# Attention, spectral mixing and two MLPs on one core: block 0's operand and the first weight half built in the query part

## The chip, the cores and the metric

One core of a Trainium2 chip runs the whole program in one launch. The metric is the device time in microseconds (us) of that core. TensorE (PE) multiplies 128x128 weights with up to 512 columns, and its weight loads (PEld) run beside the products; VectorE (DVE), ScalarE (ACT) and GpSimd (POOL) work elementwise; SyncE (SP) issues most of the DMAs.

## The reference

The inputs are q, k, v of 4 batches, 8 heads, 576 tokens and 64 features. Three parts follow one another:

```
phi(x) = exp(h - max h) / sqrt(m),  h = x omega^T - |x|^2/2
attn   = (phi(q) (phi(k)^T v)) / (phi(q) sum phi(k) + 1e-6)
x  = attn, heads joined: 4 x 576 x 512
u  = x + real(fft over tokens and features of x)
un = (u - mean u) / sqrt(var u + 1e-6)
x  = u + relu(un w1a) w2a          w1a: 512x2048, w2a: 2048x512
u  = x + (tokens mixed by U V, rank 32)
out = u + relu(u w1b) w2b
```

All inputs are float32, and the products are made from float32 values split into a high and a low part (hi, lo), three products for one: hi.hi, lo.hi, hi.lo.

## The kernel before

The tokens stand in `uT`, 128 partitions (features) by 4 feature groups by 2304 tokens. A first loop (L907) has 46 steps `n`. Steps 0 to 17 are batches 0 and 1, steps 18 to 35 batches 2 and 3; of each 18, the first nine are key tiles (`proj`, `exps`, `kvmm`) and the last nine query tiles of 128 tokens (`qtr`, `num`, `xdiv`, `xtr`). `xdiv` divides by the denominators into `x` and writes a strided copy `xr`; `xtr` transposes it into `uT` one or two steps later. `split_in(n+3)` (L239) splits the inputs of three steps ahead into `thi` and `tlo`.

The transform of a batch is written into the same steps as pieces, by the table `PLAN` (L58): F is a fold (sums and differences of pairs of `x` tiles, then four half sums, then a split into `zh` and `zl`, where the copies and subtractions wait in the list `zpend` until `zflush`), L the fold of the shared tile, S a stage of products with cosine tables whose result is split into `abh`, `abl`, D the second stage, whose results are added into `uT` by POOL (L443). A letter g or v after a fold names the engine of its sums, of its half sums and of its `zl`.

The first MLP works on five blocks of tokens (512, 384, 512, 384, 512). A block needs its mean, its centred operand `X[(0, blk)]` as a hi and a lo tile, and the factor `RST[blk]` of its variance, which multiplies only the result. For block 0 the mean and variance are made by `ln_stats` from step 23 on, the operand by `ln_apply` (L569) in step 36: for each of four feature groups a subtraction `n` (L575), a copy `xh` (ACT, L120) and a subtraction `xl` (L121), with the engines of `LNA`. The tiles lie in a pool `xpa` that opens in step 36, where the query part's pools close. The other blocks go by generators in the list `jobs`: `prep_lna` makes the mean (`s`, `pmn`), `prep_lnb` (L607) the operand, then the variance: squares summed on POOL (L626), tiny products `pvc` (L640), root, reciprocal, products `prs`, `RST`. Each `yield` ends a tick, and `tick()` advances the first generator of `jobs` by one. `l1` and `l2` call it after every feature group, that is, every three products of a unit.

A unit is one block and 128 hidden columns: `l1(i)` makes twelve products `ph`, ReLU on ACT (`hh`) and the rest on DVE (`hl`); `l2(i)` makes twelve products into `acc`. The weights come as 64-bit integers' halves, are converted (`w_conv_a`, `conv_b`) into `W[j]`, j = 2 x column group + half, and split into `wh`, `wl` by `wsplit` (L192); `w_conv_a(j)` also issues the load of half j+1 on SP.

Steps 36 to 45 still belong to the first loop. Step 36 (s = 0) opens the pools of the MLP, calls `ln_apply(0)` and splits the first halves of weights 0 and 1 on DVE; step 37 calls `l1(0)`, splits five more halves on POOL, converts halves 6 and 7 and puts `prep_lna(1)`, `prep_lnb(1)` into `jobs`; from step 38 on `step(s - 2)` runs a unit each. After the loop all jobs are drained, `prep_lnb(2)` runs until its operand stands, and units 7 to 159 follow.

In the first loop a planner orders the instructions of each engine by its own simulation, with the program's order as priority; `tc.issue_after(i)` puts the instructions made in it, on the engine of `i`, behind `i`. From unit 7 on (`manual_schedule`) each engine runs in the order of the program.

Of the kernel before, what the change touches and what calls it, by code (L numbers as in the profile page):

```python
# [47 lines left out]
LNA = 'gvvgvgvg'  # L48
# [27 lines left out]
        (13, "aF0evvv aF0ovvg"),  # L76
# [17 lines left out]
def tile_favor_fnet_moe(ctx: ExitStack, tc: tile.TileContext, qT, kT, v1, om, w1a, w2a, uu, vv, w1b, w2b, cs, cd, out):  # L94
# [24 lines left out]
    def split(dst_hi, dst_lo, src, lo_eng):  # L119
        nc.scalar.activation(dst_hi, src, AF.Copy)  # L120
        lo_eng.tensor_tensor(out=dst_lo, in0=src, in1=dst_hi.bitcast(F32), op=ALU.subtract)  # L121
# [70 lines left out]
    def wsplit(fi, k, e=nc.gpsimd):  # L192
# [3 lines left out]
        pool = wpools[0 if slot < 4 else 1]  # L196
# [9 lines left out]

    ca = ExitStack()
# [7 lines left out]
    NS = 36  # L215
    raw_, hl_, vt_, phi_, pj_, kvp_, kv_, qpT_, pn_, x_, xr_ = ({} for _ in range(11))
# [56 lines left out]
    def exps(n, g):  # L273
        if n >= NS:
            return
        pss, mx = pj_[n]
        for hh in range(4):
            h = 4 * g + hh
            nc.scalar.activation(phi_[n][:, h, :], pss[g][:, hh, :], AF.Exp, bias=mx[:, h : h + 1])  # L279
# [83 lines left out]
    def fold(src, key, eng, zeng):  # L363
        z = plf.tile([128, 4, 128], F32, tag="z", name=f"z{key}", bufs=2)
        e2 = lnt("sa", f"e2{key}")[:, 0:256]
# [26 lines left out]
    def s_stage(b, kd, kind):  # L392
# [16 lines left out]
        split(abh[:, :, c0 : c0 + w], abl[:, :, c0 : c0 + w], pv, nc.vector)  # L409
# [55 lines left out]
    def zflush(k=9):  # L465
        for _ in range(min(k, len(zpend))):
            zpend.pop(0)()
# [94 lines left out]
    def x_tiles(nm, blk):  # L562
        nb = BLKS[blk][1]
        pool = xps[0 if blk < 2 else 1]
# [4 lines left out]
    def ln_apply(blk, seng, eng):  # L569
# [3 lines left out]
        for r in range(4):  # L573
            c = lnt("ct", f"n{blk}_{r}")[:, 0:nb]
            seng[r].tensor_tensor(out=c, in0=uT[:, r, c0 : c0 + nb], in1=mean, op=ALU.subtract)  # L575
            split(hi[:, r, :], lo[:, r, :], c, eng[r])
# [8 lines left out]
    def prep_lna(blk):  # L585
# [4 lines left out]
        s2 = lnt("sb", f"s2_{blk}")[:, 0:nb]  # L590
# [4 lines left out]
        for _ in range(5 if blk > 2 else 2):  # L595
# [11 lines left out]
    def prep_lnb(blk):  # L607
# [24 lines left out]
        X[(0, blk)] = hi, lo  # L632
        yield
        for _ in range(5):
# [210 lines left out]
    jobs, wjobs = [], []  # L845
# [8 lines left out]
    def tick():  # L854
        turn[0] += 1
        advance(jobs)
        if turn[0] % 2 or len(wjobs) > 2:
            advance(wjobs)

    def step(i):  # L860
# [3 lines left out]
        if i == TAIL:  # L864
            jobs.append(lnb2)
# [41 lines left out]
    for n in range(NS + 10):  # L907
        s = n % 18
        pieces = fill.get(n, [])
        if n < NS:  # L910
# [10 lines left out]
            split_in(n + 3)  # L921
            if n == LNS:
# [35 lines left out]
        else:  # L958
            if s == 0:
# [10 lines left out]
                ln_apply(0, [eng[e] for e in LNA[0:4]], [eng[e] for e in LNA[4:8]])  # L970
                wsplit(0, 0, nc.vector)
                wsplit(1, 0, nc.vector)
            if s == 1:
                xtr(n - 2)
                l1(0)
                wsplit(0, 1)
                wsplit(1, 1)
                wsplit(2, 0)
                wsplit(2, 1)
                for j in (6, 7):  # L980
                    conv_b(*w_conv_a(j), nc.gpsimd)
# [115 lines left out]
```

## Time and profile before

| | us |
|---|---|
| median of 3 runs | 1080.05 |
| lowest, highest | 1078.63, 1084.92 |
| profiled execution, its time | 1079.91 |
| its span | 1078.1 |
| mean granted clock of PE | 0.991 |

The span goes from the first instruction to the last; the time around it is 1.8 us more. The granted clock is a share of the full 2.4 GHz; the other level is 1.2 GHz, so a stretch that shows 0.66 ran part of the time at the one and part at the other. "A <- B: 1.9, 1, 1.9" in a list of waits says that A waited for B, 1.9 us in total, once, at most 1.9 us. Spans on POOL are rough.

### The profile page before, as it was taken

How to read it: one execution, taken by the hardware profiler on the slowest of the kernel's cores; microseconds unless marked ns; L12 is line 12 of the kernel's file. 1: busy time of each engine (PE TensorE's matmuls, PEld its weight loads, DVE VectorE, ACT ScalarE, POOL GpSimd, SP SyncE). 2: the span in 40 equal slices, each digit the busy share in tenths (PEclk: the TensorE clock that was granted, in tenths of full speed). 3: DMA queues.
4: the chain of work that ended last, by engine and by line, in shares of the span. 5: the costliest groups of instructions: out<-in, count | busy, mean ns of one | idle time of the engine just before them, and what ended most of it. 6: DMA issues, size and time to landing. Idle time of an engine off the chain costs nothing.

```text
span 1078.1 us, 14786 instructions
## 1 busy us (share of the span) xinstructions
PE 1048.5 (97%) x5704; PEld 925.8 (86%) x5704; DVE 582.0 (54%) x1023; ACT 400.2 (37%) x894; POOL 414.3 (38%) x386
## 2 busy tenths in 40 slices
PE   8999998889889999999999999999999999999998
PEld 7989998679788889898889787789898989888996
DVE  6798788785488653445336656562433334332222
ACT  7877786543344231322222435331312132131110
POOL 2467755765436434634445246230410140131000
PEclk9999998989999999999999999999999999999999
DMA  7642320100012120111011101111111011100111
GB/s 241 195 143 54 105 60 1 40 1 1 1 59 84 48 87 21 40 59 49 30 40 59 40 1 40 39 40 40 40 43 56 20 46 52 59 1 1 69 40 69
DMA packets 47590, 56.87 MB, mean 53 GB/s; under 512 B 3040, under 2 KB 39264, under 8 KB 47392
## 3 DMA queue, kind: packets, MB, share of 16 engines
q1 hardware_dynamic: 47232, 53.23, 15.9%
q0 software_dynamic: 288, 2.70, 0.7%
q8 instruction: 45, 0.74, 0.3%
q14 instruction: 25, 0.20, 0.1%
HBM read 51.20 MB, written 4.72 MB: 52 GB/s over the span
## 4 chain that ended last, share of the span: by engine, by line
PE 87%; DVE 6%; POOL 4%; issue 1%; ACT 1%; DMA 0%; DVEq 0%; SPq 0%; POOLq 0%; ACTq 0%
PE ph L775 12%; PE ph L777 12%; PE ph L776 12%; PE acc L796 12%; PE acc L798 11%; PE acc L797 11%; PE kvp L290 3%; PE pn L327 2%; PE pj L263 1%; POOL uT L443 1%; PE pj L264 1%; PE pj L265 1%; PE pt L311 1%; POOL s L626 1%; PE mt L710 1%
## 5 line engine op out<-in xcount | busy, mean ns | idle before, releaser
L782 DVE SCALAR_TENSOR_TENSOR hl<-ph,hh 128x512 fp32r<-128x512 f32 (+1 forms) x160 | 101.9, 637 | 360.1 <-ACT hh L781 359.7
L781 ACT ACTIVATE hh<-ph 128x512 fp32r<-128x512 f32 (+1 forms) x160 | 88.9, 555 | 509.1 <-PE ph L777 508.7
L796 PE MATMUL acc<-hh,wh 128*128 128x512 f32 (+1 forms) x640 | 238.5, 373 | 0.0
L798 PE MATMUL acc<-hl,wh 128*128 128x512 f32 (+1 forms) x640 | 237.1, 371 | 0.5 <-DVE hl L782 0.5
L797 PE MATMUL acc<-hh,wl 128*128 128x512 f32 (+1 forms) x640 | 236.9, 370 | 0.0
L808 POOL TENSOR_TENSOR uT<-uT,t 128x512 f32<-128x512 f32 (+1 forms) x80 | 99.2, 1271 | 136.5 <-DVE t L807 136.5
L158 POOL TENSOR_TENSOR w<-mc,sc 128x512 uint32<-128x512 uint32 x48 | 62.9, 1310 | 213.6 <-DVE mc L155 206.9
L798 PEld LDWEIGHTS acc<-hl,wh 128*128 128x128 f32 x640 | 120.5, 188 | 17.5 <-DVE hl L782 1.4
L796 PEld LDWEIGHTS acc<-hh,wh 128*128 128x128 f32 x640 | 120.7, 189 | 17.1 <-issue 0.9
L797 PEld LDWEIGHTS acc<-hh,wl 128*128 128x128 f32 x640 | 120.7, 189 | 15.5
L775 PE MATMUL ph<-xh,wh 128*128 128x512 f32 (+1 forms) x320 | 122.3, 382 | 0.0
L776 PE MATMUL ph<-xl,wh 128*128 128x512 f32 (+1 forms) x320 | 119.9, 375 | 1.9 <-DVE xl L121 1.9
L777 PE MATMUL ph<-xh,wl 128*128 128x512 f32 (+1 forms) x320 | 119.7, 374 | 0.5 <-DVE wl L121 0.5
L775 PE MATMUL ph<-yh,wh 128*128 128x512 f32 (+1 forms) x320 | 118.7, 371 | 0.0
L777 PE MATMUL ph<-yh,wl 128*128 128x512 f32 (+1 forms) x320 | 118.6, 371 | 0.0
L776 PE MATMUL ph<-yl,wh 128*128 128x512 f32 (+1 forms) x320 | 118.5, 370 | 0.0
L834 POOL TENSOR_TENSOR wl<-w,wh 128x512 fp32r<-128x512 f32 x56 | 75.7, 1371 | 75.2 <-ACT wh L832 64.4
L279 ACT ACTIVATE phi<-pj,mx 128x128 f32<-128x128 f32 x288 | 82.2, 385 | 10.9 <-DVE mx L268 10.1
L776 PEld LDWEIGHTS ph<-xl,wh 128*128 128x128 f32 x320 | 60.8, 190 | 10.6 <-DVE xl L121 2.4
L775 PEld LDWEIGHTS ph<-xh,wh 128*128 128x128 f32 x320 | 60.8, 190 | 9.4 <-issue 1.4
L777 PEld LDWEIGHTS ph<-xh,wl 128*128 128x128 f32 x320 | 60.8, 190 | 9.1 <-DVE wl L121 0.8
L777 PEld LDWEIGHTS ph<-yh,wl 128*128 128x128 f32 x320 | 60.1, 188 | 8.2
(644 smaller groups left out, 1765.6 us busy)
## 6 DMA issues: line engine op xcount, KB each, us to landing
raw<-in_w1a_dram SPq DMA_DIRECT2D x16, 512.0 KB, 3.6
raw<-in_w2a_dram SPq DMA_DIRECT2D x16, 512.0 KB, 3.5
raw<-in_w1b_dram SPq DMA_DIRECT2D x16, 512.0 KB, 3.6
raw<-in_w2b_dram SPq DMA_DIRECT2D x16, 512.0 KB, 3.6
vt<-in_v_dram SPq DMA_DIRECT2D x18, 260.0 KB, 4.2
raw<-in_qT_dram SPq DMA_DIRECT2D x18, 256.0 KB, 3.2
raw<-in_kT_dram SPq DMA_DIRECT2D x17, 256.0 KB, 3.1
out_dram<-uT SPq DMA_DIRECT2D x11, 256.0 KB, 2.2
```

Source lines behind the costliest of these rows:

```text
L158: aeng.tensor_tensor(out=dst.bitcast(U32), in0=mu, in1=s, op=ALU.add)
L279: nc.scalar.activation(phi_[n][:, h, :], pss[g][:, hh, :], AF.Exp, bias=mx[:, h : h + 1])
L775: nc.tensor.matmul(ph, wh[:, c], xh[:, r, :], start=(r == 0), stop=False)
L776: nc.tensor.matmul(ph, wh[:, c], xl[:, r, :], start=False, stop=False)
L777: last[0] = nc.tensor.matmul(ph, wl[:, c], xh[:, r, :], start=False, stop=(r == 3)).ins
L781: nc.scalar.activation(hh, ph, AF.Relu)
L782: nc.vector.scalar_tensor_tensor(out=hl, in0=ph, scalar=0.0, in1=hh.bitcast(F32), op0=ALU.max, op1=ALU.subtract)
L796: nc.tensor.matmul(a[r], wh[:, c], hh, start=(q == 0), stop=False)
L797: nc.tensor.matmul(a[r], wl[:, c], hh, start=False, stop=False)
L798: last[0] = nc.tensor.matmul(a[r], wh[:, c], hl, start=False, stop=(q == GRP - 1)).ins
L808: nc.gpsimd.tensor_tensor(out=u, in0=u, in1=t, op=ALU.add)
L834: nc.gpsimd.tensor_tensor(out=lo, in0=src, in1=hi.bitcast(F32), op=ALU.subtract)
```

## The change

Block 0's operand, and the first weight half of slot 0, get a pool `xp0` of their own that is open from the start. `ln_apply` becomes a generator that does one feature group in each of steps 30 to 33, all on POOL; `wsplit(0, 0)` runs in step 34 on POOL. `l1(0)` moves from step 37 to the end of step 36, and `wsplit(1, 0)` from step 36 to 37. The conversion of halves 6 and 7 and the splits of weight 3 move to step 38, with their DVE part behind the last `abl`. One fold of batch 2 moves from step 31 on DVE to step 30 on POOL, and `zflush` issues behind the last exponential. Two scratch sums change their buffers (`sq`, two of them, in place of `sa` and `sb`, one each). For blocks 3 and 4, `prep_lna` pauses three ticks before its sums and three more after them. The variance of a block becomes a generator of its own, `prep_rs`, in a second list `jobs2`, that is advanced beside `jobs`, with 9 pauses in place of 6.

```diff
-LNA = 'gvvgvgvg'
+LNA = 'gggggggg'
...
-        (13, "aF0evvv aF0ovvg"),
+        (12, "aF0oggg"),
+        (13, "aF0evvv"),
...
     def wsplit(fi, k, e=nc.gpsimd):
...
-        pool = wpools[0 if slot < 4 else 1]
+        pool = xp0 if slot + k == 0 else wpools[0 if slot < 4 else 1]
...
+    xp0 = ctx.enter_context(tc.tile_pool(name="xp0", bufs=1))
     ca = ExitStack()
...
-        e2 = lnt("sa", f"e2{key}")[:, 0:256]
+        e2 = lnt("sq", f"e2{key}")[:, 0:256]
...
-    def zflush(k=9):
-        for _ in range(min(k, len(zpend))):
-            zpend.pop(0)()
+    def zflush():
+        with tc.issue_after(lexp[0]) if n + 1 < NS else ExitStack():
+            while zpend:
+                zpend.pop(0)()
...
     def x_tiles(nm, blk):
         nb = BLKS[blk][1]
-        pool = xps[0 if blk < 2 else 1]
+        pool = xp0 if blk == 0 else xps[0 if blk < 2 else 1]
...
     def ln_apply(blk, seng, eng):
...
         for r in range(4):
+            yield
             c = lnt("ct", f"n{blk}_{r}")[:, 0:nb]
...
     def prep_lna(blk):
...
-        s2 = lnt("sb", f"s2_{blk}")[:, 0:nb]
+        s2 = lnt("sq", f"s2_{blk}")[:, 0:nb]
+        for _ in range(3 if blk > 2 else 0):
+            yield
...
-        for _ in range(5 if blk > 2 else 2):
+        for _ in range(8 if blk > 2 else 2):
             yield
...
         X[(0, blk)] = hi, lo
-        yield
-        for _ in range(5):
+        jobs2.append(prep_rs(blk, s3))
+        yield
+
+    def prep_rs(blk, s3):
+        nb = BLKS[blk][1]
+        for _ in range(9):
             yield
...
     def tick():
         turn[0] += 1
         advance(jobs)
+        advance(jobs2)
...
         if i == TAIL:
-            jobs.append(lnb2)
+            jobs.insert(0, lnb2)
...
             split_in(n + 3)
+            if n == 29:
+                lna0 = ln_apply(0, [eng[e] for e in LNA[0:4]], [eng[e] for e in LNA[4:8]])
+                next(lna0)
+            if 29 < n < 34:
+                next(lna0, None)
+            if n == 34:
+                wsplit(0, 0)
...
-                ln_apply(0, [eng[e] for e in LNA[0:4]], [eng[e] for e in LNA[4:8]])
-                wsplit(0, 0, nc.vector)
-                wsplit(1, 0, nc.vector)
             if s == 1:
                 xtr(n - 2)
-                l1(0)
-                wsplit(0, 1)
-                wsplit(1, 1)
-                wsplit(2, 0)
-                wsplit(2, 1)
-                for j in (6, 7):
-                    conv_b(*w_conv_a(j), nc.gpsimd)
-                wsplit(3, 0)
-                wsplit(3, 1)
+                if 1:
+                    wsplit(1, 0, nc.vector)
+                    wsplit(0, 1)
+                    wsplit(1, 1)
+                    wsplit(2, 0)
+                    wsplit(2, 1)
                 jobs.extend([prep_lna(1), prep_lnb(1)])
             zflush()
             for p in pieces:
                 p()
+            if s == 0:
+                l1(0)
+            if s == 2:
+                with tc.issue_after(labl[0]):
+                    for j in (6, 7):
+                        conv_b(*w_conv_a(j), nc.gpsimd)
+                wsplit(3, 0)
+                wsplit(3, 1)
...
-    while jobs:
+    while jobs or jobs2:
         tick()
```

Here `lexp` is the last exponential made and `labl` the last `abl`.

## Rows read from the trace of the kernel before

**Rows 1.** The page's first part: busy time, share of the span and instructions of each engine.

```profile
PE 1048.5 (97%) x5704; PEld 925.8 (86%) x5704; DVE 582.0 (54%) x1023; ACT 400.2 (37%) x894; POOL 414.3 (38%) x386
```

**Rows 2.** Busy time by stretch: stretch, length, engines (count), PE's granted clock, DMA, GB/s.

```profile
155.00:190.00 35.00, 31.98 (x257) 30.35 (x255) 28.92 (x73) 24.05 (x66) 16.44 (x20) 0.90 0.01 2
...
150.00:190.00 40.00, 36.98 (x297) 34.94 (x296) 33.22 (x87) 29.01 (x78) 16.98 (x21) 0.91 0.01 2
190.00:215.00 25.00, 19.96 (x108) 16.60 (x106) 17.92 (x32) 12.88 (x26) 20.57 (x21) 0.93 0.13 42
...
226.00:236.00 10.00, 7.26 (x23) 5.82 (x22) 8.53 (x18) 3.60 (x6) 6.48 (x8) 0.66 0.00 0
...
270.00:281.00 11.00, 7.97 (x36) 6.31 (x35) 3.53 (x6) 0.86 (x2) 7.01 (x7) 0.84 0.00 0
...
300.00:340.00 40.00, 36.77 (x187) 31.88 (x187) 38.23 (x55) 19.28 (x35) 21.51 (x15) 1.00 0.29 85
```

**Rows 3.** What PE's products waited for, whole span: total us, times, longest us.

```profile
PE pvc L640 <- POOL s L626: 7.1, 3, 3.0
...
PE pt L311 <- ACT phi L279: 3.6, 3, 1.6
PE ph L776 <- DVE xl L121: 1.9, 1, 1.9
PE ps_3o L402 <- DVE abl L121: 1.8, 1, 1.8
...
PE pmn L598 <- DVE s L594: 1.4, 1, 1.4
...
PE pdq2r L425 <- DVE den L336: 0.7, 1, 0.7
```

**Rows 4.** A wait of ACT in 190 to 215 us.

```profile
ACT xh L120 <- PE pn L327: 1.4, 1, 1.4
```

**Rows 5.** POOL's groups by shape in 190 to 236: busy us, mean ns, idle before.

```profile
L121 POOL TENSOR_TENSOR wl<-w,wh 128x512 fp32r<-128x512 f32 x6 | 9.0, 1514 | 0.0
...
L121 POOL TENSOR_TENSOR xl<-n,xh 128x512 fp32r<-128x512 f32 x2 | 2.6, 1282 | 1.9 <-ACT xh L120 1.9
L575 POOL TENSOR_TENSOR n<-uT,mean 128x512 f32<-128x512 f32 x1 | 1.7, 1732 | 0.0
```

**Rows 6.** POOL's groups by shape in 155 to 190.

```profile
L386 POOL TENSOR_TENSOR eo_1e<-x,x 128x512 f32<-128x512 f32 x1 | 1.3, 1271 | 0.4 <-DVE z2o L367 0.4
L575 POOL TENSOR_TENSOR n<-uT,mean 128x512 f32<-128x512 f32 x1 | 1.3, 1262 | 0.0
L367 POOL TENSOR_TENSOR z2l<-x 128x256 f32<-128x256 f32 x1 | 0.8, 789 | 0.1
...
L366 POOL TENSOR_TENSOR e22o<-eo_1o 128x256 f32<-128x256 f32 x1 | 0.7, 723 | 0.3 <-DVE z2o L369 0.3
...
L369 POOL TENSOR_TENSOR z2o<-e22o 128x128 f32<-128x128 f32 x1 | 0.4, 445 | 0.0
```

**Rows 7.** DVE in order of time: start us, duration us, line, instruction.

```profile
161.50 0.39 DVE L367 TENSOR_TENSOR z2e<-eo_0e 128x256 f32<-128x256 f32 x1
...
166.40 1.51 DVE L367 TENSOR_TENSOR z2o<-eo_0o 128x256 f32<-128x256 f32 x1
...
169.32 0.68 DVE L268 TENSOR_REDUCE mx<-pj 128x4 f32<-128x512 f32 x1
```

**Rows 8.** POOL in order of time, beside the DVE rows above.

```profile
166.15 1.47 POOL L246 TENSOR_TENSOR tlo<-raw,thi 128x512 fp32r<-128x512 f32 x1
```

**Rows 9.** POOL in order of time, first and last ahead of `pvc` of block 1.

```profile
218.34 1.45 POOL L626 TENSOR_TENSOR s<-s,q 128x384 f32<-128x384 f32 x1 [2.66 <-ACT q L624]
...
226.22 2.70 POOL L626 TENSOR_TENSOR s<-s,q 128x384 f32<-128x384 f32 x2
```

**Rows 10.** The chain that ended last, 180 to 345: start us, us, what.

```profile
264.23 4.77 POOL uT L443 x7
...
285.04 0.23 PE ph L776
```

More of the change, by code (lines that the diff above doesn't have):

```diff
@@ L119, in split @@
     def split(dst_hi, dst_lo, src, lo_eng):
-        nc.scalar.activation(dst_hi, src, AF.Copy)
-        lo_eng.tensor_tensor(out=dst_lo, in0=src, in1=dst_hi.bitcast(F32), op=ALU.subtract)
+        hi = nc.scalar.activation(dst_hi, src, AF.Copy).ins
+        return hi, lo_eng.tensor_tensor(out=dst_lo, in0=src, in1=dst_hi.bitcast(F32), op=ALU.subtract).ins
     def conv_a(dst, raw, c0, n, p, nm):
@@ L215, in tile_favor_fnet_moe @@
     NS = 36
+    lexp, lxh, labl = [None], [None], [None]
     raw_, hl_, vt_, phi_, pj_, kvp_, kv_, qpT_, pn_, x_, xr_ = ({} for _ in range(11))
@@ L278, in exps @@
             h = 4 * g + hh
-            nc.scalar.activation(phi_[n][:, h, :], pss[g][:, hh, :], AF.Exp, bias=mx[:, h : h + 1])
+            lexp[0] = nc.scalar.activation(phi_[n][:, h, :], pss[g][:, hh, :], AF.Exp, bias=mx[:, h : h + 1]).ins
     def kvmm(n):
@@ L408, in s_stage @@
         pv = ps[:, 0 : 2 * w].rearrange("p (a s) -> p a s", a=2)
-        split(abh[:, :, c0 : c0 + w], abl[:, :, c0 : c0 + w], pv, nc.vector)
+        labl[0] = split(abh[:, :, c0 : c0 + w], abl[:, :, c0 : c0 + w], pv, nc.vector)[1]
     DST = {
@@ L573, in ln_apply @@
         for r in range(4):
+            yield
             c = lnt("ct", f"n{blk}_{r}")[:, 0:nb]
             seng[r].tensor_tensor(out=c, in0=uT[:, r, c0 : c0 + nb], in1=mean, op=ALU.subtract)
-            split(hi[:, r, :], lo[:, r, :], c, eng[r])
+            lxh[0] = split(hi[:, r, :], lo[:, r, :], c, eng[r])[0]
         X[(0, blk)] = hi, lo
@@ L827, in sjob @@
         slot = fi % RING
-        pool = wpools[0 if slot < 4 else 1]
+        pool = xp0 if slot + k == 0 else wpools[0 if slot < 4 else 1]
         hi = pool.tile([128, 512], F32R, tag=f"wh{slot}_{k}", name=f"wh{fi}_{k}")
@@ L844, in tile_favor_fnet_moe @@
                 wq_at.setdefault(PER * g + 15 + q, []).append(lambda fi=GRP * (g + 1) + q, k=k: sjob(fi, k))
-    jobs, wjobs = [], []
+    jobs, jobs2, wjobs = [], [], []
     turn = [0]
```

## The prediction

> **What bounds the kernel now.** I read the page's first part, then busy time by stretches, then what TensorE (PE) waits for, then the stretches around those waits. PE is busy 97% of the span [rows 1], so the program is worth what PE loses by standing still or by running at half clock. A stretch loses its length minus its busy time, plus its length times (1 minus the granted clock). By the table of stretches [rows 2] that is, in us: A, 150 to 190, the end of the query part: 3.0 idle + 0.09 x 40 = 3.6 of clock = 6.6. B, 190 to 215, the first weight units: 5.0 + 0.07 x 25 = 1.8, 6.8. C, 226 to 236: 2.7 + 0.34 x 10 = 3.4, 6.1. D, 270 to 281: 3.0 + 0.16 x 11 = 1.8, 4.8. E, 300 to 340: 3.2, no clock. Together 27.5; what is lost elsewhere the edits don't touch. The clock of a whole stretch is a mix of 1.2 and 2.4 GHz; in A, C and D the low level stands right behind a gap of PE, so I count it with the gap.
>
> The reader should next see who ends these gaps. `pvc` (L640) waits 7.1 us in three places for the squares' sum `s` on POOL (L626): the longest, 3.0, is D's whole idle time, C's is 2.7, which leaves 1.4 for E. The transposes `pt` wait 3.6 for the exponentials, the longest, 1.6, in A; in B it is `ph` for `xl` (1.9), `ps_3o` for `abl` (1.8), `pdq2r` (0.7); in E also `pmn` for the sum `s` (1.4) [rows 3]. PE takes its instructions in order, so each of these held everything behind it.
>
> **The change, part by part.** The profiled execution took 1079.9 us around a span of 1078.1; the runs' median is 1080.05, 0.1 above. The sum is made against 1079.9.
>
> *B: the operand and first weight half built early, +4.0.* Before, `xh`/`xl` of block 0 live where the query part's tiles lay: the first ACT copy waits 1.4 us for the last `pn` product [rows 4], and four subtractions, four copies, four `xl` and the first `wl` crowd behind it. The new home is free all along, so the chain runs in steps 30 to 33 and 34, and l1(0), now one step earlier, finds its operands. From this stretch POOL loses two `xl` of 1.3 and one `n` of 1.7 [rows 5], DVE one `n`, two `xl` and one `wl`. The sums of block 1 and folds get their own `sq` buffers in place of `sa`/`sb`, which can only remove waits. The conversion of halves 6 and 7 goes one step later and on DVE behind the last `abl`: that is the 1.8 us before `ps_3o`. It moves two 512 KB loads (7, 8) by one step on SP, where nothing urgent stands behind them, and delays the splits of unit 3, which l1(3) needs two steps later; I cost that at nothing, covered by two steps of products. The waits named, 4.4 of the 5.0, could all go, and the clock's 1.8 with them. What is late next: `wl` of half (0,1) on POOL and (1,0) on DVE, 1.5 each or more, of which I leave one and a half, or 2.8 us. Bounds 0 (the operand comes late after all) to 6.8; near the upper end, because the waits removed are named ones.
>
> *A: the price of it, +1.0.* POOL was busy 16.4 of the 35 us from 155 to 190 [rows 2]. Added: three `n` of 1.3 to 1.7 (one already lies there), four `xl` of 1.3, one `wl` of 1.5 [rows 5], and batch 2's fold 0o taken from DVE: 1.3 + 0.7 + 0.8 + two of 0.4 [rows 6]; 4.5 + 5.1 + 1.5 + 3.6 = 14.7. That makes 31.1 of 35, so it fits, barely, and `tlo` and `xr`, which the next projections and transposes need, now queue behind it. For it DVE, busy 28.9 of 35, drops the five fold instructions and one `n`. They matter: the row maxima that release the exponentials stood behind them; `mx` started only at 169.3, behind a `z2o` of 1.51 us that takes 0.39 when alone [rows 7], and PE stood for 1.6 us. The copies of fold results now issue behind the last exponential of the next tile, which takes them out of the way of the `pt` waits. ACT gets five copies more and idles 10.9 of these 35 us; nothing. Upper bound +6.6 (the whole loss); lower bound -14.7, all added POOL time on the path. I take 1.0, nearer the upper end, since 4 us of POOL stay free.
>
> Here row and rule agree on the hardware and disagree with the edit. The stretched `z2o` [rows 7] ran while POOL's `tlo` held from 166.15 to 167.62, and ended 0.3 us after it [rows 8]: a DVE sum of two SBUF operands waits a POOL operation out.
> The Trainium skill, SBUF — State Buffer, section Who interferes with whom, says so as a rule: such a DVE instruction and a GpSimd one that reads SBUF exclude each other, and the later one stands for the whole of the other. By it, moving work to POOL would not relieve DVE, and A would lose rather than win; that is the slower rival below.
>
> *C: `pvc` of block 1 later, +3.0.* The second moment's products come after 9 pauses in a queue of their own, not 6 in the common one. One tick is three 128x512 products, 3 x 0.23 = 0.69 us [rows 10]; three ticks are 2.1. POOL works without a hole from 218.3 to 228.9, twelve instructions: `s`, a fold sum, eight `uT` additions, two `s` [rows 9], so the wait of 2.7 drops to 0.6, and with a short gap I take 0.9 of the clock's 3.4 back. Bounds 0 (POOL just as late, since PE arrives earlier) to 6.1.
>
> *D: the same for block 2, +4.0.* Here the order is written out: before, `pvc` falls at the sixth tick of the main loop, now at the tenth: 2.8 us later against a wait of 3.0 [rows 3, 10]. The chain ahead of it (seven `uT` additions of 4.8 us, then `s`) hangs on PE's own products, so it doesn't slip. 2.8 and 1.2 of the clock. Bounds 2.8 to 4.8.
>
> *E: sums of blocks 3 and 4, +2.0.* By counting pauses: block 4's sums come at tick 28, not 31, its `pmn` at 37 as before; its `pvc` at tick 57, not 54. Three ticks, 2.1 us, cover either wait of 1.4. Against it, block 3's operand is complete at tick 24, not 18, exactly when l1(12) asks for it, and DVE is 38.2 of 40 busy in E [rows 2]: I take off 0.8. Bounds 0 to 3.2.
>
> Sum: 1.0 + 4.0 + 3.0 + 4.0 + 2.0 = 14.0; 1079.9 - 14.0 = 1065.9, so **1066**.
>
> **Rivals.**
> *POOL becomes the bound of the query part (slower).* Place: steps 30 to 34, POOL at 31.1 of 35. If its 14.7 us land on the path (late `xr`, late `tlo`, and DVE's own folds stretched as 0.39 to 1.51 [rows 7]), the operand of block 0 is late as well and B and C give nothing: 1079.9 + 14.7 - 6.0 = 1088.6. It decides from where more than 11 of the 14.7 show. For it: POOL's load by steps is uneven: 155 to 190 holds six steps, 5.8 us each, and steps 30 and 32 each get `n`, `xl` and a whole fold, over 6 us, beside `tlo`. Against: 18.6 of POOL's 35 us were free, and a planner that knows POOL as an engine makes the order. 9 in 100. The skill's rule above is this rival's ground.
> *The gaps move.* PE comes sooner, POOL and DVE don't: DVE is busy 8.5 of 10 us in C and 17.9 of 25 in B [rows 2]. Then A, B and C give 0 on balance, D and E 6.0: 1073.9. For it: C's DVE share. Against: the removed work is theirs. 16 in 100.
> *The early build isn't early.* The planner may put POOL's new instructions behind its older ones, the operand comes after 190, and what D and E win is spent on PE's new order in A: 1078, no change. 11 in 100.
> *Everything fits.* B to E lose nothing (20.9) and A wins 3: 1056. 12 in 100.
>
> **How the numbers follow.** The forecast has 52 in 100. A measurement here tells about 0.5% (5.4 us) from no change: faster is below 1074.7, slower above 1085.5. Faster: 52 + 12 + two thirds of the moved gaps (10) = 0.74; same: the rest of them (6) and the early build that isn't (11) = 0.17; slower 0.09. The range goes from 1056, where everything fits, to 1077: A at -5, B 3, C 0, D 4, E 1.
>
> **What would show it.** Right: `xl` and `n` of block 0 on POOL between 155 and 190; no wait of `ph` for `xl` or of `ps_3o` for `abl`; `pvc` waits near 0.6, 0.2 and 0; granted clock 1.0 where D stands. Wrong: PE waiting for `xr`, `tlo` or fold results of POOL before 190; a wait of l2(0) or l1(1) for `wl` above 3 us; `pvc` waits unchanged in C; l1(12) waiting for block 3's `xl`. Any of the first two of these above 5 us breaks the forecast.

## The result, and the profile after

The changed kernel takes 1095.3 us (1094.2 to 1098.51, 4 runs) against 1081.51 beside it (1078.63 to 1084.92, 4 runs): a ratio of 1.0135 [1.01, 1.017], so 1.35% slower, where 14 us less had been forecast and the range ended at 1077. The profiled execution took 1094.53 us around a span of 1092.8, 14.7 more than the span of before.

The page's first part of the changed kernel, busy time by engine, answers to [rows 1]:

```profile
PE 1057.8 (97%) x5704; PEld 933.6 (85%) x5704; DVE 574.9 (53%) x1013; ACT 398.3 (36%) x894; POOL 423.6 (39%) x396
```

PE is busy 9.3 us longer with the same 5704 products: that is products at a lower clock, and the other 5.4 us of the loss are standing still. From 130 us on the changed kernel is 10 to 17 us behind, so the stretches of [rows 2] lie later in it. Busy time by stretches: A's part of the program, D's part, and a stretch that [rows 2] doesn't have (stretch, length, PE, weight loads, DVE, ACT, POOL, granted clock, DMA, GB/s):

```profile
166.00:206.00 40.00, 32.50 (x261) 30.34 (x260) 27.43 (x75) 28.02 (x77) 26.83 (x30) 0.91 0.01 4
...
284.00:295.00 11.00, 10.68 (x54) 9.03 (x54) 7.97 (x13) 3.65 (x7) 9.82 (x10) 1.00 0.00 0
...
50.00:150.00 100.00, 92.84 (x707) 88.92 (x706) 76.69 (x156) 64.61 (x185) 61.41 (x74) 0.91 0.30 91
```

The last row is the one that matters, and no stretch on which the prediction rests lies in it. In the kernel before the same hundred microseconds, and ten of them, are:

```profile
50.00:150.00 100.00, 98.36 (x820) 95.25 (x819) 84.85 (x177) 76.81 (x219) 70.95 (x89) 1.00 0.34 105
120.00:130.00 10.00, 10.00 (x78) 9.52 (x77) 6.89 (x12) 7.72 (x24) 5.12 (x8) 1.00 0.54 173
```

In the hundred, 820 against 707 products, and a clock of 1.00 against 0.91: the key part of the last two batches, which no part of the change was meant to touch. What PE waits for, whole span (total us, times, longest), against [rows 3]:

```profile
PE pj L266 <- ACT phi L282: 5.3, 4, 2.7
PE kvp L293 <- ACT phi L282: 4.7, 1, 4.7
...
PE acc L809 <- DVE hl L793: 3.7, 2, 3.2
PE acc L807 <- ACT hh L792: 3.2, 1, 3.2
PE pn L330 <- ACT qpT L116: 2.8, 1, 2.8
...
PE pvc L651 <- POOL s L633: 0.3, 1, 0.3
```

The waits of before that the change aimed at are gone: `pvc` 7.1 to 0.3, `ph` for `xl`, `ps_3o` for `abl`, `pmn` for `s`. Others stand in their place: `kvp` 4.7 in one piece, `hl` 3.2, `hh` 3.2, `pn` 2.8, and `pj` for `phi` with 2.7 in one piece. The 4.7 is worth following. The timeline around it, DVE, POOL, ACT and the one late product (start, us, engine, line, operation; in brackets the idle time before and who ended it):

```profile
105.31 0.65 ACT L116 ACTIVATE zh1o<-z1o 128x512 fp32r<-128x512 f32 x1
...
105.83 0.65 ACT L116 ACTIVATE zh1e<-z1e 128x512 fp32r<-128x512 f32 x1
...
107.18 0.98 DVE L384 TENSOR_TENSOR zl1o<-z1o,zh1o 128x512 fp32r<-128x512 f32 x1
...
108.09 0.98 DVE L384 TENSOR_TENSOR zl1e<-z1e,zh1e 128x512 fp32r<-128x512 f32 x1
108.60 1.62 POOL L510 TENSOR_TENSOR s<-uT 128x512 f32<-128x512 f32 x1
109.00 1.51 DVE L370 TENSOR_TENSOR z1e<-eo_1e 128x256 f32<-128x256 f32 x1
110.30 1.33 POOL L511 TENSOR_TENSOR s<-s,s 128x512 f32<-128x512 f32 x1
110.43 1.35 DVE L371 TENSOR_TENSOR z1e<-e21e 128x128 f32<-128x128 f32 x1
111.59 1.31 POOL L249 TENSOR_TENSOR tlo<-raw,thi 128x512 fp32r<-128x512 f32 x1
111.70 1.35 DVE L372 TENSOR_TENSOR z1e<-e21e 128x128 f32<-128x128 f32 x1
...
112.97 1.23 DVE L139 CUSTOM_DVE_ANT_0 w<-mc,sc 128x1024 uint16<-128x1024 uint16 x1
...
114.12 1.87 DVE L271 TENSOR_REDUCE mx<-pj 128x4 f32<-128x512 f32 x3
...
114.89 1.14 ACT L282 ACTIVATE phi<-pj,mx 128x128 f32<-128x128 f32 x4 [6.86 <-DVE mx L271]
115.31 1.26 PE L293 MATMUL kvp<-vt,phi 64*128 64x65 f32 x6 [4.71 <-ACT phi L282]
```

Read from the bottom: PE waits for the exponential `phi`, that for the row maxima `mx`, and three of those are done only from 114 to 116, behind five DVE instructions of folds and one of a conversion. The folds stand there because their copies `zh1o` and `zh1e` on ACT were held back until 105.3 and 105.8. In the kernel before, `zh1e` of the same fold starts at 96.4, and two sums `z1e` of the next fold ran alone, 0.28 us each at 101.0 and 101.6; of the two, the first is shown:

```profile
96.35 0.62 ACT L115 ACTIVATE zh1e<-z1e 128x512 fp32r<-128x512 f32 x1
...
101.04 0.28 DVE L368 TENSOR_TENSOR z1e<-e21e 128x128 f32<-128x128 f32 x1
```

Here each of them takes 1.35, the one beside POOL's `s`, the other beside its `tlo`. The three sums `z1e` take 4.2 us here and 1.0 before (0.42 + 0.28 + 0.28), so by these rows an estimated 3 of the 4.7 us are DVE sums stretched beside POOL. Three later stretches of the changed kernel show what the gap cost after it had ended (same columns as the stretches above):

```profile
115.00:120.00 5.00, 4.69 (x19) 4.17 (x20) 3.40 (x6) 4.13 (x14) 1.14 (x1) 0.57 0.67 218
120.00:130.00 10.00, 10.00 (x39) 8.54 (x38) 0.60 (x2) 2.65 (x8) 1.26 (x1) 0.50 0.00 0
130.00:140.00 10.00, 10.00 (x69) 9.52 (x67) 5.20 (x11) 5.64 (x16) 3.11 (x5) 0.86 0.37 107
```

From 120 to 130 PE has no hole and runs at 1.2 GHz: 39 products, where before there are 78.

To see where the time went I made a ledger: the start of the first product of each projection and each first-layer unit, this kernel's minus before's. It comes from the timelines alone, to some tenths. The rows used below are in one table with the runs that matter (us; positive is later than before):

| at (time before, us) | changed | run 1 | run 2 | run 5 | run 7 | run 10 | run 17 | run 18 |
|---|---|---|---|---|---|---|---|---|
| projection 23 (109) | 0.0 | 1.6 | 1.6 | -0.9 | 0.9 | 2.3 | 1.2 | -0.1 |
| projection 26 (130) | 13.3 | 1.6 | 14.8 | -0.9 | 0.9 | 2.3 | 1.2 | -0.1 |
| projection 35 (172) | 15.9 | 6.9 | 14.8 | -0.7 | 4.3 | 5.7 | 4.5 | -0.2 |
| l1(1) (212) | 10.2 | 1.6 | 12.5 | -3.1 | -6.8 | -5.1 | -6.3 | 1.1 |
| l1(3) (224) | 11.9 | 3.2 | 12.5 | -1.6 | -5.1 | -3.3 | -4.5 | 1.8 |
| l1(5) (250) | 16.8 | 6.4 | 12.5 | 0.1 | 0.1 | 0.8 | -0.5 | 4.5 |
| l1(9) (277) | 12.0 | 1.7 | 13.0 | -4.6 | -4.6 | -3.9 | -5.3 | -0.1 |
| l1(12) (296) | 12.5 | 2.1 | 12.5 | -4.1 | -4.1 | -3.5 | -4.8 | 0.3 |
| l1(15) (313) | 10.8 | 0.4 | 12.5 | 1.6 | -5.8 | -0.3 | -5.2 | -0.2 |
| l1(17) (326) | 14.1 | 3.8 | 12.5 | -1.0 | 0.2 | -1.8 | -6.4 | -0.8 |
| l1(20) (343) | 13.7 | 3.3 | 12.5 | -0.6 | -0.2 | -0.1 | -4.4 | 0.7 |

The changed kernel's column is the whole story in signs: it loses 13.3 at 110, 2.6 by the end of the projections, wins 5.7 up to l1(1), loses 6.6 up to l1(5), wins 4.8 at l1(9), loses 1.7 up to l1(20), and 1.0 more lies behind that: 14.7.

Each column is one execution, and executions of one kernel differ by several microseconds. Runs 5 and 18 issue the same instructions in the same order on PE, DVE, ACT and POOL up to 278 us, and their columns still differ by 4.2 at l1(1) and 4.4 at l1(5). So a difference of this size between 172 and 250 us is not shown by two columns alone; there the times decide.

### The profile page after: what moved, and what is told of

Its sections match the earlier page's. It is cut to its first block, busy times and chain, and to the rows that moved or that the text cites. A ratio compares the mean times of both kernels' runs of the same rounds, so it can differ in the third digit from the quotient of the medians.

```text
span 1092.8 us, 14775 instructions
## 1 busy us (share of the span) xinstructions
PE 1057.8 (97%) x5704; PEld 933.6 (85%) x5704; DVE 574.9 (53%) x1013; ACT 398.3 (36%) x894; POOL 423.6 (39%) x396
## 4 chain that ended last, share of the span: by engine, by line
PE 84%; DVE 8%; POOL 4%; issue 2%; ACT 2%; DMA 0%; DVEq 0%; SPq 0%; ACTq 0%; POOLq 0%
PE acc L809 11%; PE ph L786 11%; PE acc L807 11%; PE ph L788 11%; PE ph L787 11%; PE acc L808 11%; PE kvp L293 3%; PE pn L330 2%; PE pj L266 1%; PE pj L268 1%; PE pj L267 1%; POOL uT L446 1%; ACT phi L282 1%; PE mt L721 1%; PE pt L314 1%
```

## The experiments

### Runs 1 to 4: which edit makes the gap at 110

Three parts could have made it: the rule on the fold copies (Z), the shared sums' new buffers (S), or POOL's early build of block 0's operand pulling on the whole order (P).

**Run 1**, the changed kernel with the rule taken out:

```diff
     def zflush():
-        with tc.issue_after(lexp[0]) if n + 1 < NS else ExitStack():
-            while zpend:
-                zpend.pop(0)()
+        while zpend:
+            zpend.pop(0)()
```

> The changed kernel with the fold copies no longer issued behind the last exponential (zflush as before). Theory Z (that rule delays zh, zl and then z1e, which land on DVE ahead of the maxima mx at 109 to 114 us and start 20 us of half clock): the gap of 4.7 us before kvp at 110 to 115 goes and projections 24 and 25 come back by 11 to 13 us; time 1078 to 1084. Theory S (the second scratch buffer for the folds' half sums does it): no change, 1093 to 1097. Theory P (the early build on POOL does it): no change, 1093 to 1097.

Measured 1084.45 us (1082.77 to 1086.85, 10 runs) beside 1081.97 of before, ratio 1.0028 [1.0015, 1.0041]. The stretch that had lost is back, here 50 to 150 and 120 to 130 of run 1:

```profile
50.00:150.00 100.00, 96.08 (x790) 91.94 (x789) 84.01 (x172) 74.45 (x215) 72.02 (x88) 1.00 0.32 99
...
120.00:130.00 10.00, 10.00 (x79) 9.52 (x79) 6.21 (x11) 7.22 (x22) 4.71 (x6) 1.00 0.51 164
```

**Run 2**, the kernel before with that rule alone put in:

```diff
-    def zflush(k=9):
-        for _ in range(min(k, len(zpend))):
-            zpend.pop(0)()
+    def zflush():
+        with tc.issue_after(lexp[0]) if n + 1 < NS else ExitStack():
+            while zpend:
+                zpend.pop(0)()
```

> The kernel before with that one rule added (fold copies behind the last exponential) and nothing else. Theory Z: the gap appears at 110 us and the half clock after it, 1091 to 1096 against 1081 before. Theories S and P: within 3 us of the kernel before.

Measured 1092.93 (1091.95 to 1097.38, 4 runs), ratio 1.0115 [1.0087, 1.0144]. PE's longest wait from 50 to 150 in run 2, and the same stretch as above:

```profile
PE kvp L291 <- ACT phi L280: 4.7, 1, 4.7
```

```profile
120.00:130.00 10.00, 10.00 (x37) 8.38 (x37) 2.22 (x4) 3.30 (x11) 1.54 (x2) 0.50 0.00 0
```

The same wait, of the same 4.7 us, and the same low clock, with nothing else of the change in the kernel. So Z is shown from both sides: the rule alone makes 12.5 us at l1(20) of run 2, and without it the changed kernel is 10.9 us faster (13.8 over its kernel before against 2.5).

**Run 3**, the changed kernel with the sums back in their old buffers:

```diff
-        e2 = lnt("sq", f"e2{key}")[:, 0:256]
+        e2 = lnt("sa", f"e2{key}")[:, 0:256]
...
-        s2 = lnt("sq", f"s2_{blk}")[:, 0:nb]
+        s2 = lnt("sb", f"s2_{blk}")[:, 0:nb]
```

> The changed kernel with the half sums of the folds and the block sums back in their single buffers sa and sb. Theory S: 1079 to 1085. Theories Z and P: the gap at 110 us stays, 1092 to 1098.

Measured 1101.1 (1100.01 to 1103.97, 4 runs), ratio 1.0183 [1.0163, 1.0203]: slower still. S falls, and the new buffers are worth some 5 to 6 us in this kernel.

**Run 4**, the changed kernel with block 0's operand and first weight half built in step 36 as before, on the engines of before, in the new home:

```diff
-            if n == 29:
-                lna0 = ln_apply(0, [eng[e] for e in LNA[0:4]], [eng[e] for e in LNA[4:8]])
-                next(lna0)
-            if 29 < n < 34:
-                next(lna0, None)
-            if n == 34:
-                wsplit(0, 0)
...
                 wpools.append(mp)
+                for _ in ln_apply(0, [eng[e] for e in LNA[0:4]], [eng[e] for e in LNA[4:8]]):
+                    pass
+                wsplit(0, 0, nc.vector)
```

> The changed kernel with block 0's operand and first weight half built in step 36 again, on the engines of before, but in the new home. Theory P: 1078 to 1085. Theories Z and S: the loss before 140 us stays; what the early build is worth shows alone between 150 and 225 us: if it gains 4 there, 1097 to 1100; if it costs, 1090 to 1093.

Measured 1094.97 (1091.89 to 1100.13, 4 runs), ratio 1.0127 [1.0091, 1.0163], the changed kernel's time. P falls as the cause of the loss at 110: without the early build `kvp` waits the same 4.7 us, and the loss at projection 26 is whole (18.4, in an execution that was the longest of the four).

### Runs 5 to 8: the parts one by one

**Run 5**, the kernel before with the second queue alone (`prep_rs` and `jobs2` as in the change, and the blocks' `s2` in `sq`, which it needs; `prep_lna`'s pauses as before).

> The kernel before with one part of the change alone: the second moment's products and what follows them in a queue of their own with 9 pauses (and the sums of blocks 1 to 4 in their own buffer, which it needs). Theory D: this part earns what D showed in the changed kernel's ledger (4.4 us between l1(8) and l1(10)) and C's 1.5 to 2.7, and the waits that came in their place (acc for hh at 240 us, acc for hl before l1(16)) belong to other parts: 1075 to 1078, no wait of pvc above 0.6, no wait of acc above 1. Rival: those waits come with this queue itself, since its copies and square roots run beside the sums: 1079 to 1083, pvc's waits gone and a wait of acc for hh or hl of 2.5 us or more.

Measured 1083.65 (1079.16 to 1086.41, 12 runs), ratio 1.0019 [1.0002, 1.0036]; the profiled execution was one of the shorter, 1079.38. A miss, and the rival's picture. D's gain is there (0.1 to -4.6 between l1(8) and l1(9)), `pvc` waits 0.3, but from 285 to 345 PE waits in new places (`hh` 1.5 and the row below), and by l1(20) 4.0 of the 4.6 is gone:

```profile
PE acc L802 <- DVE hl L786: 3.2, 2, 2.4
```

**Run 6**, run 1 with the old pauses of blocks 3 and 4 (0 and 5, not 3 and 8).

> The first experiment's kernel (the changed one with the fold copies free) with the old pauses of blocks 3 and 4 (0 ahead of the sums and 5 behind, in place of 3 and 8). Theory: the six extra pauses bring block 4's operand onto ACT and DVE exactly where unit 15 needs hh and hl; with the old ones the wait of acc for hl (3.2 us before l1(16)) falls below 1 and the time to 1081 to 1082. Rival: the second queue and the conversions beside it make that wait: it stays above 2.5 us, and the time within 1 us of 1084.5. A third: block 4's sums come late again for pmn (1.4 us before), and nothing is won.

Measured 1087.47 (1086.82 to 1089.37, 4 runs), ratio 1.0064 [1.0044, 1.0084]: 3 us worse than run 1, so the six pauses help. They are too few, not too many, which run 5 shows as well.

**Run 7**, run 1 with the build late (run 4's edit).

> The first experiment's kernel with block 0's operand and first weight half built in step 36 on the engines of before (the new home stays). Theory: the early build costs about as much in the query part (5.1 us between projections 26 and 32 in the first experiment's ledger) as it wins in the first weight units (6.9): projection 32 and l1(0) back within 2 us of before, l1(1) within 2 us of the first experiment, the time 1083 to 1087. Rival 1: the loss in the query part has another cause (POOL's fold), and the early build is a pure win: 1089 or more. Rival 2: it is a pure loss: below 1082.

Measured 1080.42 (1076.16 to 1082.29, 10 runs), ratio 0.9983 [0.9966, 1.0001], below run 1's interval: the early build is a loss of about 4 us, my second rival of that run. Of PE's two longest waits in run 1 between 150 and 190 us, `pj` for `phi` and `pn` for `qpT`, 2.7 each, neither is left in run 7. In the ledger run 7 is 2.6 ahead of run 1 at projection 35 and 8.4 ahead at l1(1).

**Run 8**, run 1 with the early build, but on the engines of before (`LNA = 'gvvgvgvg'`), and the fold 0o of batch 2 back on DVE in step 13.

> The first experiment's kernel with the operand still built in steps 30 to 34, but on the engines of before (three of four subtractions and two lower halves on DVE, the others on POOL), and batch 2's fold 0o back in step 13 on DVE. Theory P2: the 5.1 us lost in the query part are POOL's added load (the stretch from 150 to 190 has it busy 33 of 40 us in the changed kernel); with it off POOL, projection 32 is within 3 us of before and the time 1080 to 1082. Rival: any early copies and subtractions cost it, on whichever engine, by the row maxima and exponentials queued behind them: within 1.5 us of 1084.5. A third: DVE, busy 29 of these 35 us before, becomes late: 1087 or more.

Measured 1083.95 (1082.33 to 1086.71, 10 runs), ratio 1.0028 [1.0013, 1.0043], as run 1: the rival. At projection 35 it is 11.5 behind before, more than run 1's 6.9, so the price of the early build isn't POOL's load as such; on DVE it costs as much.

### Runs 9 to 12: the burst at 300 us, and the last folds

Run 7 wins 4.7 at l1(9) and is level with before at l1(17). Its stretches from 310 to 320 show why (columns as above):

```profile
310.00:315.00 5.00, 1.82 (x7) 1.60 (x6) 4.93 (x7) 2.42 (x5) 2.10 (x2) 0.74 0.00 0
315.00:320.00 5.00, 5.00 (x19) 4.71 (x18) 2.79 (x6) 0.22 (x2) 0.00 (x0) 0.50 0.69 201
```

One gap of 3.2 us in the first row, then five microseconds without a hole at 1.2 GHz. Run 7's timeline ahead of the gap:

```profile
309.67 1.46 DVE L636 TENSOR_TENSOR xl<-c,xh 128x512 fp32r<-128x512 f32 x1
...
311.40 0.65 ACT L146 ACTIVATE sc<-raw 128x512 uint32<-128x512 uint32 x1
311.50 1.38 DVE L152 TENSOR_SCALAR mc<-mc 128x512 uint32<-128x512 uint32 x1
311.96 0.46 ACT L791 ACTIVATE hh<-ph 128x384 fp32r<-128x384 f32 x1
312.80 0.55 DVE L792 SCALAR_TENSOR_TENSOR hl<-ph,hh 128x384 fp32r<-128x384 f32 x1
...
313.40 0.69 PE L808 MATMUL acc<-hl,wh 128*128 128x384 f32 x1 [3.18 <-DVE hl L792]
```

`hh` and `hl` of unit 15, which PE needs, stand behind block 4's operand (`xl`) and a weight conversion (`mc`, `sc`). The changed kernel has the same order with the same numbers 17 us later: `mc` 1.38, `hh` 0.46, a wait of 3.19.

**Run 9**, run 7 with `hh` and `hl` issued ahead of the unit's last tick in the written-out part (`if r < 3 or i < TAIL: tick()`, and the fourth tick behind `hl`).

> The seventh experiment's kernel (fold copies free, block 0's operand built late: 1080.4) with hh and hl of a unit of the written-out part issued ahead of the unit's last tick, not behind it. Theory E1: the wait of acc for hl before l1(16), 3.2 us with some 4 us of low clock behind it, is one of place in the queue: four ACT and three DVE instructions of block 4's operand and of the weight conversion stand ahead of hh and hl of unit 15; with a tick less ahead of them the wait falls below 1.5 and the time to 1074 to 1077. Rival: DVE is simply full there (14.8 of 15 us from 300 to 315), so what is put ahead delays the operand or the weights instead: PE waits for xl, wl or w by as much, and the time stays at 1079 to 1081.

Measured 1088.52 (1086.14 to 1090.69, 10 runs), ratio 1.0064 [1.004, 1.0088], 8 us slower than run 7. The wait of 3.2 is gone (in its place 1.7 of `prs` for `rc` and 1.6 of `hl` elsewhere), and units 17 and 18 come out 1.5 ahead of run 7's and l1(20) level with it (-0.2); the 8 us are lost between l1(66) and l1(86), around the end of the first layer, where the same edit reorders the jobs. The edit was too wide; for the stretch in question the rival holds.

**Run 10**, run 7 with 8 pauses ahead of block 4's sums, not 3.

> The seventh experiment's kernel with 8 pauses, not 3, ahead of block 4's sums. Theory E2: the second queue brought block 4's sums and operand forward (its first sum ends at 296 here, at 308 before), into unit 15; five ticks later (some 3.5 us) the conversion and the operand no longer meet there, the wait of 3.2 falls below 1.5 and the time to 1074 to 1077. Rival: DVE is full over the whole stretch, and the wait only changes its name (xl of block 4 before l1(16), or hl of the next unit): 1079 to 1082.

Measured 1080.55 (1079.69 to 1084.37, 10 runs), ratio 0.9998 [0.9975, 1.0021]. The rival, in its own words: the wait changed its name. Run 10's timeline:

```profile
301.66 1.75 DVE L597 TENSOR_TENSOR s<-uT 128x512 f32<-128x512 f32 x1
303.33 0.68 DVE L598 TENSOR_TENSOR s<-uT 128x512 f32<-128x512 f32 x1
304.04 0.69 DVE L600 TENSOR_TENSOR s<-s,s 128x512 f32<-128x512 f32 x1
304.65 0.17 DVE L655 RECIPROCAL rc<-rc 128x3 f32<-128x3 f32 x1
...
304.88 1.65 PE L661 MATMUL prs<-ident,rc 128*128 128x128 f32 x6 [3.18 <-DVE rc L655]
```

Block 4's three sums now stand ahead of block 3's reciprocal, an instruction of 0.17 us, and PE waits 3.18 for it.

**Run 11**, run 7 with the last batch's folds one step earlier:

```diff
-        (20, "aS3e aS3o"),
-        (21, "aDr1 bF0egvv"),
-        (22, "bF0ovvv bF1evvg bF1ovgv"),
+        (20, "aS3e aS3o bF0egvv"),
+        (21, "aDr1 bF0ovvv bF1evvg bF1ovgv"),
```

> The seventh experiment's kernel with the last batch's four folds issued one step earlier. Theory C: what is gained up to l1(3) (5 us ahead of before) is given back at l1(5) because these folds run at the same time as before on DVE, which works without a hole from 209 to 232; issued a step earlier they use DVE's and POOL's holes around 200 to 209, the waits of acc for hh (2.5) and of ps_0e for zl3e (2.0) shrink, and l1(5) keeps 2 us or more of the 5: 1076 to 1079. Rival: the folds hang on DVE's own order or on the last x tiles, l1(5) comes out as before and the time stays within 1 us of 1080.4. A third: they delay the splits and sums of units 0 to 2 and the time rises above 1082.

Measured 1081.43 (1076.57 to 1085.72, 10 runs), ratio 0.9993 [0.9967, 1.0019]. The waits for `hh` and `zl3e` shrink (2.5 to 1.0; gone), but `pvc` waits 3.6 and `pdq2r` 2.5 instead, and l1(5) is 3.6 late: nothing won, and C's cause is not settled by it.

**Run 12**, both edits of runs 9 and 11.

> The two edits, hh and hl ahead of the last tick and the folds a step earlier, together on the seventh experiment's kernel. If E1 and C both hold, their gains add: 1070 to 1075, under both kernels. If only E1 holds, 1074 to 1077 as without the folds; if only C holds, 1076 to 1079. Rival: what C gains makes PE arrive earlier at block 4's operand and the wait there grows by the same: no better than the better of the two alone.

Measured 1092.44 (1089.29 to 1093.7, 6 runs), ratio 1.0098 [1.0061, 1.0136]: run 9's loss, with nothing from run 11.

### Runs 13 to 16: is it the conversions

**Run 13**, run 7 with the conversions of the second group's weights started two units earlier (`10 + q` becomes `8 + q` for the first group). **Run 16** is its control, the same edit on the kernel before.

> The seventh experiment's kernel (fold copies free, operand built late) with the conversion of the second group's weight halves started at unit 8, not 10. Theory E3: DVE has too much to do from 300 to 315 us (14.8 of 15: block 2's epilogue, block 4's sums and operand, conversions of 2.2 us a half), and that burst gives back what D won; two units earlier, five halves less stand in it, in a stretch where DVE has room (255 to 281: 14 of 26 us busy). Then no wait over 1.5 us between l1(13) and l1(18), units 17 to 19 stay 3 us or more ahead of before, and the time is 1075 to 1078. Rival: the burst is of the epilogue and the operand, or something behind unit 17 sets the pace whatever comes before; units 17 to 19 come out within 1 us of before, and the time is 1079 to 1082.

> The kernel before with the conversions started at unit 8 alone, as a control. By E3 it wins little here, since its waits in that stretch are of block 4's sums (1.4 and 1.4 us), not of the conversions: 1078 to 1081, and its wait of pvc for block 2 (3.0 us) stays. Rival: an earlier conversion wins by itself (under 1077), so what E3 gains has nothing to do with the change; or it delays the second moment further (POOL and ACT are in both) and costs: over 1083.

Run 13: 1083.9 (1081.85 to 1086.43, 10 runs), ratio 1.0017 [1.0, 1.0034]. Run 16: 1085.1 (1083.32 to 1089.75, 10 runs), ratio 1.0039 [1.0025, 1.0054]. Both lose 4 to 5 us between l1(18) and l1(19), at a new wait for `hl` of 3.4; up to l1(18) run 13 is 1.2 ahead of run 7. The conversions are not what gives the gain back, and an earlier start costs by itself.

**Run 14**, run 7 with the fold 0o back on DVE in step 13.

> The seventh experiment's kernel with batch 2's fold 0o back on DVE in step 13 (the plan of before). Theory Q: the 4.3 us that it lost by the end of the projections come from that fold on POOL, ahead of xr and tlo (a wait of px for xr of 2.4 us); with the old plan the last projection is within 1.5 us of before and l1(1) 8 us or more ahead of it. But l1(5) comes out as before, as the folds of the last batch set it, so the time changes by less than 1.5 us from 1080.4. Rival: the price comes with the sums' and subtractions' new buffers or the order of the fold copies: last projection still 3 us or more late, l1(1) no earlier.

Measured 1080.53 (1079.0 to 1084.79, 10 runs), ratio 0.9994 [0.9979, 1.0009]. Half right: the wait of `px` for `xr` of 2.4 is gone, and from projection 23 to 35 run 14 loses 1.0, where run 7 loses 3.4; the time didn't change, as expected. But the last projection is 4.9 late, 2.4 of it since projection 8, ahead of anything that the edit touches, and l1(1) was 0.4 late, not 8 early, with `ph` waiting 2.1 for `xl`; that profiled execution was the longest of the ten, so I don't lean on its ledger.

**Run 15**, runs 13 and 14 together.

> Both edits on the seventh experiment's kernel: conversions started at unit 8 and the fold 0o back on DVE in step 13. By E3 and Q together: units 5 to 9 as before, then 4 us won at l1(9) and kept: 1074 to 1077, under both kernels. Rival: no better than before (1079 to 1082), since the end of the first layer is set by the burst whatever its parts.

Measured 1085.97 (1085.45 to 1088.87, 6 runs), ratio 1.0046 [1.0028, 1.0064]: run 13's loss again.

### Runs 17 and 18: both instructions ahead of the burst

**Run 17**, run 7 with 11 pauses ahead of block 4's sums and 6 behind, so that neither `hl` of unit 15 nor block 3's reciprocal stands behind them:

```diff
-        for _ in range(3 if blk > 2 else 0):
+        for _ in range({3: 3, 4: 11}.get(blk, 0)):
...
-        for _ in range(8 if blk > 2 else 2):
+        for _ in range({3: 8, 4: 6}.get(blk, 2)):
```

> The seventh experiment's kernel with block 4's sums 8 pauses later, not 5 (run 10), and 6 pauses, not 8, behind them: block 3's reciprocal is then issued ahead of the sums that held it for 3.2 us in run 10. Theory E4: in every variant one DVE instruction that PE waits for stands behind some 3 us of block 4's work or the conversion's, and that single wait, with the low clock behind it, takes back D's gain; ordered so that neither the reciprocal (l1(14)) nor hl (l1(16)) stands there, units 14 to 18 stay 3 us or more ahead of before and the time is 1075 to 1078. Rival: DVE is full from 300 to 320 whatever the order, so the wait takes a third name (pmn, or xl of block 4 at l1(16)), units 17 to 19 come out within 1 us of before, and the time is 1079 to 1082.

Measured **1077.01** (1075.08 to 1079.28, 12 runs) beside 1080.99, ratio 0.996 [0.9942, 0.9978]: 4 us under the kernel before, as expected, and 18 under the changed one. Against run 7 it is 3.4 by the medians and 2.5 by the ratios; the shortest executions of run 7, from 1076.2 on, are as short as its own. Its stretches from 300 to 325:

```profile
300.00:305.00 5.00, 4.25 (x24) 3.56 (x23) 4.97 (x9) 1.63 (x3) 1.49 (x1) 1.00 0.09 30
305.00:310.00 5.00, 5.00 (x28) 4.60 (x27) 4.93 (x10) 2.69 (x5) 0.35 (x1) 1.00 0.33 107
310.00:315.00 5.00, 5.00 (x27) 4.51 (x26) 5.00 (x7) 4.55 (x9) 3.71 (x3) 1.00 0.32 105
315.00:320.00 5.00, 3.83 (x24) 3.43 (x23) 4.90 (x10) 1.22 (x3) 0.57 (x1) 1.00 0.24 80
320.00:325.00 5.00, 3.40 (x18) 2.55 (x17) 4.56 (x7) 1.84 (x3) 4.80 (x4) 1.00 0.41 134
```

DVE is full from end to end (24.4 of 25 us; 19.6 in run 7, where it stood still behind PE's gap), so the rival's premise is true and its conclusion false. PE still stands in three of the five stretches, 3.5 us in all, in pieces of 1.6 and less, and the clock stays at 1.00.

**Run 18**, run 5 (the kernel before with the second queue) with run 17's pauses.

> The kernel before with the second queue alone, as in the fifth experiment (1083.7), and the pauses of run 17 (3 and 8 for block 3, 11 and 6 for block 4): nothing of the fold rule, of the new home or of the early build. By E4: D's 4 us stay in the sum: 1075 to 1078, the same as run 17, since what the first units win is given back by l1(5). Rival: 1080 to 1084, the wait under another name.

Measured 1079.83 (1076.73 to 1082.67, 12 runs), ratio 0.9987 [0.997, 1.0003]: no difference from before that can be measured, but 3.8 by the medians, 3.5 by the ratios, under run 5, which has the old pauses. Most of D's gain stays up to the end here too (4.5 at l1(5), -0.1 at l1(9), 0.7 at l1(20)), so E4 holds in this kernel as well. The forecast of the same time as run 17 was wrong: six of the twelve executions lie with run 17's (1076.7 to 1079.0), six higher (1080.7 to 1082.7), and the profiled one is of the higher. It is 4.5 behind at l1(5), where run 5, in the same order up to there, is 0.1 behind; so its ledger doesn't say what the new home and the new order of the first weight units are worth. By the times of these two runs they are worth 2.8 us, together with whatever else the two kernels differ in; how is open.

## Why the prediction was wrong

**The step that failed** is the sentence in part A, "The copies of fold results now issue behind the last exponential of the next tile, which takes them out of the way of the `pt` waits", together with "what is lost elsewhere the edits don't touch". `zflush` is called in every step, not only in those of stretch A. I priced the rule in the one place where it looked good and at nothing in the others. In the key part it holds the copies back on ACT, and what hangs on the copies, the `zl` subtractions and the next fold's sums on DVE, is then issued ahead of the row maxima of the next tiles: a wait of 4.7 us and some 17 us at the low clock. Runs 1 and 2 give its size, 10.9 us out of the changed kernel and 11.0 into the old one (1092.93 against 1081.97 beside it). None of the rivals named this place; the slower one (POOL becomes the bound, 1088.6) had the right sign, and what it describes shows in A, but the larger loss lies elsewhere.

This step isn't the whole miss. The ledger is off from the forecast by 28.7 us (14.0 won against 14.7 lost): 13.3 are this rule, 9.6 C, 3.7 E, 3.6 A and 1.0 behind l1(20), and B and D came out 1.7 and 0.8 above their terms. Without the rule, run 1 still took 1084.45, where 1066 had been forecast.

**A, +1.0 forecast.** Lost 2.6 in the changed kernel (13.3 to 15.9), 5.3 in run 1. In A's part of the program POOL is busy 26.8 of 40 us, against 17.0 before: 9.8 more, where 14.7 had been counted. The term that failed is "ACT gets five copies more and idles 10.9 of these 35 us; nothing". In the changed kernel one of these copies stood on ACT ahead of exponentials that PE needed:

```profile
190.05 0.63 ACT L121 ACTIVATE xh<-n 128x512 fp32r<-128x512 f32 x1 [4.43 <-POOL n L580]
190.59 1.12 ACT L282 ACTIVATE phi<-pj,mx 128x128 f32<-128x128 f32 x4
...
191.76 0.39 PE L266 MATMUL pj<-omh,thi 128*128 128x256 f32 x1 [2.71 <-ACT phi L282]
```

POOL, without a hole from 181 to 193, started `n` only at 188.8; the maxima for `phi` had been ready since 184.7. Run 1 has the same wait of 4.43 and the same 2.7 on PE, run 7 neither. What I wrote of `xr` queued behind POOL's work came as well: in run 7, which still has the fold 0o on POOL, `px` waits 2.4 for `xr`, and in run 14, which hasn't, this wait is gone. That the build itself belongs early is refuted: run 7 against run 1 makes it a loss of 4 us, and run 8 makes it one on the old engines too.

**B, +4.0 forecast.** The waits named are gone and the changed kernel wins 5.7 from projection 35 to l1(1). But the reason I gave, the operand built early, isn't it: run 7 builds it late and wins 11.1 over the same way (4.3 to -6.8; 10.8 in runs 10 and 17). What is left for it are the free home and the new order of l1(0) and the splits, which no run takes apart.

**C, +3.0 forecast.** `pvc` of block 1 no longer waits (2.7 before), as said, and yet 6.6 was lost from l1(1) to l1(5). The rival "the gaps move" had this: PE comes sooner, DVE doesn't. ACT's line there, in the changed kernel, is the new wait:

```profile
239.86 0.63 ACT L116 ACTIVATE zh3e<-z3e 128x512 fp32r<-128x512 f32 x1 [5.01 <-DVE z3e L372]
...
241.47 0.58 ACT L792 ACTIVATE hh<-ph 128x512 fp32r<-128x512 f32 x1
...
242.09 0.79 PE L807 MATMUL acc<-hh,wh 128*128 128x512 f32 x1 [3.23 <-ACT hh L792]
```

`hh` stands in ACT's queue behind a copy that waits 5 us for a DVE fold, and the clock behind that gap was 0.52 from 246 to 256. What would free it stays open (run 11 only moved it).

**D, +4.0 forecast.** Right, in size and place: 4.8 from l1(5) to l1(9), clock 1.00 from 284 to 295, where this part now lies, and a wait of 0.3 for 3.0; 4.7 in run 5 by itself.

**E, +2.0 forecast.** Lost 3.3 from l1(15) to l1(17), and 1.7 from l1(9) to l1(20) as a whole. The count "block 4's sums come at tick 28, not 31, its `pmn` at 37 as before" was wrong: block 3's second moment no longer stands in the queue ahead of block 4's job, and six pauses don't make up for that. In run 7 the last sum ends at 296.8, where before's ends at 308.7, with PE only 5 us ahead. So the operand fell into units 14 and 15. Runs 7, 10 and 17 differ in block 4's pauses alone, and 17 keeps D's gain.

The Trainium skill, SBUF — State Buffer, section Who interferes with whom, says that a DVE instruction with two SBUF operands and a GpSimd one that reads SBUF shut each other out. The rows agree: `z1e` takes 0.28 alone and 1.35 beside POOL's `s` and `tlo`. The rival that I had put on this rule looked for it between 155 and 190; it struck at 109, since the held-back fold was moved next to POOL's `s`; in A it was POOL itself that came late.

## What to carry to other kernels

A rule put into a helper acts wherever the helper is called: price it at every call, in each stage, by what stands behind it on each engine, before its gain in the stage one has in mind. A wait removed ahead of a full engine comes back under another name; look for the short instruction that PE needs (a reciprocal of 0.17 us, an `hl` of 0.55) behind a block of work that nobody needs yet, and order that, instead of moving the block. And take the parts of a bundled change alone: of this one, the second queue is worth keeping with other pauses, and the free home with the new order of the first units seems so by runs 17 and 18; the early build and the rule are not. And before two kernels' traces are compared stage by stage, know how far two executions of one order lie apart: up to 4.4 us here.

## What the runs showed of the hardware

How long PE stays at 1.2 GHz after a gap was longer than I had counted. After the 4.7 us of 110 to 115 the granted clock was 0.57, 0.50 and 0.86 in the rows to 140, although PE had next to no hole: 2.1 + 5.0 + 1.4 = 8.5 us lost behind a gap of 4.7. After 3.2 us in run 7 it was 0.50 from 315 to 320 and 0.74 in the stretches on both sides of that. In run 17 waits of 1.6, 1.2 and 0.6 in the same place left every row at 1.00. So two kernels with nearly the same idle time differ by the clock: PE's holes from 300 to 325 are 3.2 us in run 7 and 3.5 in run 17.
